# Windowed attention with a gated feed-forward block, fp16 on one core: global key rows copied in ahead of the DMA transposes, and a reordered head

## The chip, the cores and the metric

The kernel runs on one core of a Trainium2 chip. A core has five engines that run their own instruction streams and wait for each other through semaphores: TensorE (PE, with the weight loads shown apart as PEld), VectorE (DVE), ScalarE (ACT), GpSimd (POOL) and SyncE (SP). DMA transfers are issued by SP, ACT or POOL; those that POOL issues go through one queue (q0 in the profile) and those of SP through another (q1). The metric is the device time of one execution in microseconds. All times inside the execution are counted from the start of the profiled span.

## The reference

Inputs are `q`, `k`, `v` of shape (4, 8, 768, 64) in fp32 (batch, heads, sequence, head size), and the three weights of a gated feed-forward block. Each query attends to the 8 first ("global") keys and to the 96 latest ("local") keys, with a linear distance bias for each head:

```python
rel = pos[:, None] - pos[None, :]
is_global = pos[None, :] < 8
is_local = (rel >= 0) & (rel < 96)
keep = is_global | is_local
dist = np.where(is_global & ~is_local, 96.0, np.abs(rel))
scores = q @ k.T / 8 - slopes[:, None, None] * dist      # slopes 2**-(h+1)
a = softmax(np.where(keep, scores, -1e9))
x = (a @ v) as (4 * 768, 512)
out = (silu(x @ w_gate) * (x @ w_val)) @ w_out            # d_ff 1536
```

## The kernel before, in words

**Tiling.** The four batches are called blocks 0 to 3. A block has 768 tokens in two halves of 384; each half becomes one tile `x_of(t)` of the feed-forward stage, t = 0 to 7, in which x is held transposed (feature by token). The eight heads go as four pairs `hp`; two pairs make a quad. Keys are cut into 7 chunks of 120 with their window of 216 queries. A chunk's tile has 128 columns: columns 0 to 7 hold the 8 global keys, columns 8 to 127 the 120 local ones. V has the same layout in rows (`vSs[b]`, lines 120 and 158 to 162); its rows 0 to 7 of every chunk are copied in from `vG` by SP (`copy_globals`, lines 172 to 175).

**Attention.** For each pair K and Q are needed transposed (`kT`, `qT`). Block 0 and the pairs 0 and 1 of block 1 are transposed on PE and copied out of PSUM by DVE and ACT (`transposes_half`, line 284; `transposes`, line 258); pairs 2 and 3 of block 1 and all pairs of blocks 2 and 3 are loaded as rows into `kst` and `qst` by POOL (`load_rows`, line 181) and transposed by SP's DMA (`transposes_dma`, line 391), with the last 48 keys through `kend` and `kE` (`load_ends` 188, `turn_ends` 197). Before those loads `stage(b)` (line 143) zeroes on POOL the whole of `kend` and rows 0 to 7 of `kst`. After a DMA transpose `global_keys` (line 400) copies, on POOL, the transposed global keys into columns 0 to 7 of the pair's six chunks and of `kE`. Then PE makes scores, ACT the exponentials (lines 347 and 372), DVE or POOL multiplies by `masks` (380, 383), and `Quad.weigh` (line 428 onwards, matmuls at 435) makes denominators and numerators. DVE inverts and spreads the denominators (445 to 451), ACT copies the numerators out (466) and DVE (block 0) or POOL (other blocks) scales them into x (470; 491 in the head). The masks are sixteen exponentials on ACT (`make_masks`, line 242), of 432 or 216 columns.

**Feed-forward.** For each tile t and each of the 12 blocks f of 128 hidden units, `gate_or_val` (line 513) runs 4 gate matmuls, a tanh on ACT (519) and a fused (tanh + 1) * gate on DVE into `sl` (521), then 4 value matmuls and a multiply by `sl` on DVE (525). Their PSUM banks go round a ring of three, so that a value group takes over the bank of the gate group one f before, once `sl` has been read from it. `out_part` (line 529) does 3 of the 12 output matmuls of a 128-token row block; the fourth part is evicted by ACT (543, two buffers) and stored by SP (544).

**Order.** The schedule is written out by hand: the engines' streams are filled in program order and each engine runs its stream in that order. After a head (lines 587 to 645), which does half 0 of block 0, `stretches` (line 710) lists groups of feed-forward work (gate, value or output), and between them attention steps are dealt out evenly: each group adds its weight times a quota to `owed`, and when `owed` reaches 1 the next step runs. `half1` is the second half of block 0; `first(1)` the first half of block 1, beside tile 1; `both(1)` the second half of block 1 and the first of block 2, beside tiles 2 and 3. `at_step(t, f, ...)` hangs loads and masks ahead of a gate group. Functions put off (exponentials, masks, inversions, scalings) stand in `later` and are run at the following groups. `load_w(f0, f1)` (line 205) is four POOL issues whatever its width, `load_wo(g)` one issue of 512 KB, `load_qk(b)` two of 384 KB, `load_v_rest(b, c)` one of 120 KB.

Of the kernel before, what the change touches and what calls it, by code (L numbers as in the profile page):

```python
# [16 lines left out]
WIN = 216  # L17
# [20 lines left out]
def kernel(  # L38
# [104 lines left out]
    def stage(b):  # L143
        qst[b] = sb2.tile([128, NP * J * 2 * D], FP16, name="qst", tag="qst")
        kst[b] = sb2.tile([128, NP * J * 2 * D], FP16, name="kst", tag="kst")
        kend[b] = sb2.tile([128, H, D], FP16, name="kend", tag="kend", bufs=1)
        nc.gpsimd.memset(kend[b], 0.0)
        nc.gpsimd.memset(kst[b][0:NG, 768 * (0 if b > 1 else 2):], 0.0)

    def whole(st, b):  # L150
        return st[b][:, 0:NP * J * D].rearrange("p (h x) -> p h x", h=NP)
# [1 line left out]
    def load_qk(b):  # L153
        for st, src in ((kst, k), (qst, q)):
            nc.gpsimd.dma_start(
                out=whole(st, b), in_=src[b, 0:NP].rearrange("h (p j) d -> p h (j d)", p=128))
# [6 lines left out]


    vG = sb.tile([NG, B, H, D], FP16, name="vG")

    def load_globals():
        nc.gpsimd.dma_start(
            out=vG[:, 1:].rearrange("p b h d -> p (b h) d"),
            in_=v[1:, :, 0:NG, :].rearrange("b h p d -> p (b h) d"))  # L170

    def copy_globals(b):
        nc.sync.dma_start(
# [7 lines left out]
    def load_rows(b, i, h):  # L181
        st, src = ((qst, q), (kst, k))[i]
        p0, n = (0, 128) if st is qst else (NG, KC)
        nc.gpsimd.dma_start(  # L184
            out=rows_of(st, b, h // 2)[p0:p0 + n, :, h % 2, :],
            in_=src[b, h, 0:n * J].rearrange("(t p) d -> p t d", p=n))

    def load_ends(b):
        h0 = 2 * NP - len(by_dma(b)) * 2
        nc.gpsimd.dma_start(  # L190
            out=kend[b][NG:NG + S - KC * J, h0:, :],
            in_=k[b, h0:, KC * J:S, :].rearrange("h p d -> p h d"))

    def by_dma(b):
        return range(0 if b > 1 else 2, NP)
# [9 lines left out]
    def load_w(f0, f1):  # L205
        a, z = 128 * f0, 128 * f1
        for g in range(2):
            for w, src in ((wg, moe_w_gate), (wv, moe_w_val)):
                nc.gpsimd.dma_start(
                    out=w[:, 2 * g:2 * g + 2, a:z],  # L210
                    in_=src[256 * g:256 * g + 256, a:z].rearrange("(p s) f -> p s f", s=2))
# [30 lines left out]
    def make_masks(h, c0, c1):  # L242
        nc.scalar.activation(
            out=masks[:, h, c0:c1], in_=dist[:, c0:c1], func=AF.Exp, scale=-slopes[h])
# [8 lines left out]
    class Pair:  # L253
# [143 lines left out]
                    out=dst.rearrange("r (t p) -> r t p", t=J),  # L397
                    in_=rows_of(st, b, hp).rearrange("p t e d -> p (t e d)"))

        def global_keys(self):  # L400
            k3 = self.kT.rearrange("r (c m) -> r c m", m=128)
            first = k3[:, 0, NG:2 * NG]
            nc.gpsimd.tensor_copy(
                out=k3[:, 0:J, 0:NG], in_=first.unsqueeze(1).broadcast_to([128, J, NG]))
            nc.gpsimd.tensor_copy(out=kE[:, self.hp, 0:NG], in_=first)


    class Quad:

# [158 lines left out]
    def fill(n):  # L568

        for _ in range(n):  # L570
            nc.tensor.matmul(warm[:, 0:256], lhsT=ones[:, 0:128], rhs=ones[:, 0:256],
                             start=True, stop=True)

    def p_bias(hp, which, *tags):
        pairs[0, hp].sc = pairs[0, hp].bias(0, which, [single("sc", t) for t in tags])

    def p_sc(hp, which, *tags):
        if tags:
            p_bias(hp, which, *tags)
        pairs[0, hp].scores_half(0, which, pairs[0, hp].sc)  # L580

    def p_tr(hp, kt, qt, q_eng, n_fill=0):
        tr = [single("trs", t, FP16)[:, 0:TB] for t in (qt, kt)]
        pairs[0, hp].transposes_half(0, tr, V, q_eng, lambda: fill(n_fill))

    V, A = nc.vector.tensor_copy, nc.scalar.copy
    fill(14)
    A(out=q16[:, 0, 0:2], in_=q32)
    V(out=k16[:, 0, 0:2], in_=k32)
    for h in range(4):  # L590
# [3 lines left out]
    copy_globals(0)  # L594
    for h in range(4, 8):
        make_slope(nc.vector.tensor_scalar_mul, h)
    load_w(0, 4)
    load_w(4, 6)
    load_half(1, 0, H)
    load_w(6, 8)  # L600
# [1 line left out]
    for c in range(4, NCH):  # L602
        load_v_rest(0, c)
    load_w(10, 12)
    stage(1)
    load_qk(1)
    for g in range(3):
        load_wo(g)
    load_globals()
    for c in range(4):  # L610
        load_v_rest(1, c)
    load_ends(1)
    for hp in by_dma(1):
        for i in (1, 0):
            for e in range(2):
                load_rows(1, i, 2 * hp + e)
    for c in range(4, NCH):
        load_v_rest(1, c)
    p_bias(0, 0, "a0", "a1")
    sc00 = pairs[0, 0].sc  # L620
    p_bias(0, 1, "a2", "a3")
    pairs[0, 0].scores_half(0, 0, sc00)
    p_sc(0, 1)
    p_tr(1, "x2", "o0", V)
    p_bias(1, 0, "x0", "x1")
    p_tr(2, "a0", "a1", A)
    p_sc(1, 0)
    p_sc(1, 1, "x2", "o0")
    p_tr(3, "a2", "a3", A)
    p_sc(2, 0, "a0", "a1")  # L630
    quads[0, 0].denominators(single("den", "x0"))
    p_sc(2, 1, "a2", "a3")
    for side, tag in enumerate(("x1", "x2")):
        quads[0, 0].numerators(side, single("num", tag))
    p_sc(3, 0, "a0", "a1")
    p_sc(3, 1, "a2", "a3")
    quads[0, 1].denominators(single("den", "o0"))
    for side, tag in enumerate(("x0", "x1")):
# [33 lines left out]
    def second(b):  # L672
        return [[sc(b, 0, 2), sc(b, 1, 2)], [sc(b, 2, 2), sc(b, 3, 2)],
                [va(b, 0, 1)], [va(b, 1, 1)]]
# [6 lines left out]
                pairs[b, hp].transposes_dma()  # L681
        return step

    def gk(b, *hps):
        return lambda: [pairs[b, hp].global_keys() for hp in hps]

    def first(b):
        return [[tr(b, 0), tr(b, 1), fetch(b, 2, 3)], [sc(b, 0, 0), sc(b, 0, 1)],
                [sc(b, 1, 0), sc(b, 1, 1), gk(b, 2)], [va(b, 0, 0), gk(b, 3)],
                [sc(b, 2, 0), sc(b, 2, 1)], [sc(b, 3, 0), sc(b, 3, 1)], [va(b, 1, 0)]]  # L690

    def both(b):

        n = b + 1

        return [[sc(b, 0, 2), sc(b, 1, 2)], [sc(b, 2, 2), sc(b, 3, 2), fetch(n, 0, 1)],
                [va(b, 0, 1)], [va(b, 1, 1), gk(n, 0, 1)],
                [sc(n, 0, 0), sc(n, 0, 1), fetch(n, 2, 3)], [sc(n, 1, 0), sc(n, 1, 1)],
                [va(n, 0, 0), gk(n, 2, 3)], [sc(n, 2, 0), sc(n, 2, 1)],
                [sc(n, 3, 0), sc(n, 3, 1)], [va(n, 1, 0)]]  # L700

    half1 = [[trh(0), trh(1)], [trh(2), trh(3)], [sch(0)], [sch(1)],
# [4 lines left out]
    def ff(t, f0, f1, n_out=(0,)):  # L707
        return [(t, f, n_out[(f - f0) % len(n_out)]) for f in range(f0, f1)]

    stretches = [  # L710
        (ff(0, 0, 4), [], 0),
        (ff(0, 4, 12), half1, 1.0),
        (ff(1, 0, 3) + ff(1, 3, 12, (1, 1, 2)), first(1), 6.0),
        (ff(2, 0, 12, (1,)) + ff(3, 0, 12, (1,)), both(1), 6.0),
        (ff(4, 0, 12, (1,)) + ff(5, 0, 12, (1,)), both(2), 6.0),
        (ff(6, 0, 12, (1,)), second(3), 6.0),
        (ff(7, 0, 12, (1,)), [], 0)]

    loads = {}

    def at_step(t, f, *fns):
        loads.setdefault((t, f), []).extend(fns)

    for h in range(H):
        at_step(h // 4, 1 + h % 4, lambda h=h: make_masks(h, WIN, 3 * WIN))
        at_step(h // 4, (8, 1)[h // 4] + h % 4, lambda h=h: make_masks(h, 0, WIN))
    at_step(1, 0, lambda: [copy_globals(b) for b in range(1, B)])
    for b, base, rate, v_at in ((2, 24, 2.0, (30, 31, 32, 32, 37, 38, 39)), (3, 43, 1.4, (54, 55, 56, 57, 61, 62, 63))):
        items = [(base, lambda b=b: stage(b)), (base + 1, lambda b=b: load_ends(b))]
        n = 0  # L730
# [8 lines left out]
            at_step(int(when) // NFF, int(when) % NFF, it)  # L739

    outs = [(t, i, part) for t in range(NT - 1) for i in range(3) for part in range(4)]
    for tiles, steps, tail in stretches:
        groups = []
        for t, f, n_out in tiles:
            groups += [(1.0, t, f, which) for which in range(2)]
            groups += [(1.1, t, f, 2)] * n_out
        work = sum(g[0] for g in groups)
        quota = len(steps) / (work - tail)
        owed = 0.4
        for w, t, f, which in groups:  # L750
            if which == 0:
                for ld in loads.pop((t, f), []):
                    ld()
                if f == 0:
                    run_later(len(later))
            run_later(1)
            if which == 2:
                out_part(*outs.pop(0))
            else:
                gate_or_val(t, f, which, NC if t == 0 and f < 2 else 0)  # L760
            owed += w * quota
            while owed >= 1.0 and steps:
                run_later(len(later))
                for step in steps.pop(0):
                    step()
                owed -= 1.0
        assert not steps
    assert not later and not loads and not outs
    for i in range(2):
        for part in range(4):  # L770
            out_part(NT - 1, i, part)
# [36 lines left out]
```

The softmax here doesn't subtract the row's maximum and nothing guards it: scores larger than these inputs give would overflow.

## Time and profile before

| what | value |
|---|---|
| median of 13 runs | 255.2 us (252.77 to 257.93) |
| the profiled execution | 255.31 us, span 253.5 us, mean granted clock 0.993 |
| PE busy | 239.9 us, 95% of the span |
| DVE, ACT, POOL busy | 157.7, 129.8, 127.5 us |
| DMA moved | 25.76 MB, mean 102 GB/s; 81480 of 93251 packets under 512 B |
| issue to landing, median | V chunks 7.3, kst rows 4.3, qst rows 5.1, w_out 10.8, kT and qT transposes 5.7 and 6.6 us |

A line of PE's timeline gives start, duration, engine, source line, operation, the tile written and those read, shapes, how many instructions were merged, and in brackets how long the engine stood idle ahead of it and which event ended that. The durations of matmuls overlap, so work is better read from start to start. A DMA issue on POOL shows the time that POOL took to issue it; POOL can itself be held until earlier transfers of its queue have landed, and the bracket then names one of those. The table of stretches adds the granted TensorE clock (PEclk, 1.00 is full), the DMA engines' busy share and the bytes moved.

### The profile page before, as it was taken

The page shows a single profiled execution, that of the slowest core. Times are in us where ns is not written, and L with a number is a line of the kernel's source. Part 1 is how long each engine was busy: PE and PEld are TensorE (multiplying, and loading weights), DVE is VectorE, ACT ScalarE, POOL GpSimd, SP SyncE. Part 2 cuts the span into 40 slices and gives each one's busy share as a digit, 9 for nine tenths or more (in the row PEclk, how much of TensorE's full clock was granted, in tenths as well). Part 3 has the DMA queues.
Part 4 walks back from the last instruction along what each step waited for, and adds up shares of the span by engine and source line. Part 5 has one row for each costly group of instructions (what it writes and reads, how often), then busy time and mean ns, then how long its engine had stood idle before and what let it go on. Part 6 is the DMA issues. An engine that isn't in the chain of part 4 may idle for free.

```text
span 253.5 us, 6001 instructions
## 1 busy us (share of the span) xinstructions
PE 239.9 (95%) x2380; PEld 135.1 (53%) x2380; DVE 157.7 (62%) x338; ACT 129.8 (51%) x288; POOL 127.5 (50%) x161
## 2 busy tenths in 40 slices
PE   6989998989799999979999999999999999999994
PEld 4555565545355555544555555555555565555543
DVE  4577766557665666772675666766775567555510
ACT  4736676785453744543563554455734643332321
POOL 8975995490409998918808877813020232300000
PEclk9999999999999999997999999999999999999999
DMA  8999999999711999999934999991011101101122
GB/s 160 167 192 193 178 157 191 172 130 115 134 41 44 88 152 131 173 132 99 115 56 34 113 133 181 151 121 45 0 44 41 41 3 45 41 3 41 41 83 83
DMA packets 93251, 25.76 MB, mean 102 GB/s; under 512 B 81480, under 2 KB 90280, under 8 KB 93224
## 3 DMA queue, kind: packets, MB, share of 16 engines
q0 software_dynamic: 71088, 14.00, 74.5%
q1 hardware_dynamic: 21576, 11.03, 22.7%
q8 instruction: 18, 0.29, 0.5%
q10 hardware_dynamic: 560, 0.36, 0.5%
q14 instruction: 9, 0.07, 0.1%
HBM read 28.58 MB, written 6.29 MB: 138 GB/s over the span
## 4 chain that ended last, share of the span: by engine, by line
PE 70%; DMA 16%; ACT 5%; DVE 5%; issue 2%; POOL 0%; ACTq 0%; DVEq 0%; POOLq 0%
PE ops L537 20%; PE vps L508 19%; PE gps L508 19%; DMA vS<-in_v_dram 5%; DMA kT<-kst 4%; DMA qT<-qst 3%; PE sc L364 3%; PE num L435 3%; DMA vS<-vG 2%; DVE sl L521 2%; PE den L435 2%; DMA ident<-consts 1%; ACT at L372 1%; ACT th L519 1%; PE sc L328 1%
## 5 line engine op out<-in xcount | busy, mean ns | idle before, releaser
L521 DVE SCALAR_TENSOR_TENSOR sl<-th,gps 128x384 f32<-128x384 f32 x94 | 52.0, 553 | 57.4 <-ACT th L519 56.6
L519 ACT ACTIVATE th<-gps 128x384 f32<-128x384 f32 x94 | 46.6, 496 | 65.0 <-PE gps L508 63.4
L508 PE MATMUL gps<-xT,wg 128*128 128x384 f16 x376 | 77.6, 328 | 1.6 <-DVE xT L470 1.5
L508 PE MATMUL vps<-xT,wv 128*128 128x384 f16 x376 | 77.0, 327 | 1.5 <-DVE sl L521 1.5
L537 PE MATMUL ops<-wo,hT 128*128 128x512 f16 x276 | 73.7, 382 | 0.0
L525 DVE TENSOR_TENSOR hT<-vps,sl 128x384 f16<-128x384 f32 x94 | 51.9, 552 | 9.0 <-PE vps L508 2.0
L508 PEld LDWEIGHTS <-wg 128*128 128x128 f16 x384 | 36.7, 98 | 34.8 <-issue 4.1
L508 PEld LDWEIGHTS <-wv 128*128 128x128 f16 x384 | 36.6, 98 | 27.4 <-issue 3.7
L470 POOL TENSOR_TENSOR xT<-ns,rb 128x384 f16<-128x384 f32 x24 | 24.2, 1027 | 48.2 <-DVE rb L451 47.0
L372 ACT ACTIVATE at<-sc 128x432 f16<-128x432 f32 x72 | 33.3, 534 | 11.5 <-PE sc L364 11.5
L537 PEld LDWEIGHTS <-hT 128*128 128x128 f16 x276 | 26.0, 98 | 23.9 <-issue 1.2
L160 POOL DMA_DIRECT2D vS<-in_v_dram x28 | 24.9, 899 | 1.1 <-issue 1.1
L543 ACT ACTIVATE osb<-ops 128x512 f32<-128x512 f32 x23 | 13.7, 597 | 17.7 <-PE ops L537 17.7
L184 POOL DMA_DIRECT2D kst<-in_k_dram x20 | 17.7, 900 | 4.1 <-DMA wo<-in_moe_w_out_dram 4.1
L466 ACT COPY ns<-num 128x384 f32<-128x384 f32 x28 | 12.0, 482 | 12.7 <-PE num L435 12.7
L383 DVE TENSOR_TENSOR at<-at,masks 128x864 f16<-128x864 f16 x20 | 13.0, 650 | 7.8 <-ACT at L372 7.8
L184 POOL DMA_DIRECT2D qst<-in_q_dram x20 | 17.2, 881 | 0.0
L435 PE MATMUL num<-at,vS 128*32 128x216 f16 (+6 forms) x576 | 12.5, 225 | 2.1 <-DMA vS<-in_v_dram 1.9
L383 POOL TENSOR_TENSOR at<-at,masks 128x864 f16<-128x864 f16 x4 | 7.3, 1820 | 13.3 <-ACT at L372 13.3
L347 ACT ACTIVATE at<-sc 128x432 f16<-128x432 f32 (+2 forms) x32 | 11.6, 451 | 2.9 <-PE sc L339 2.9
L435 PEld LDWEIGHTS <-vS 128*32 128x32 f16 x576 | 10.0, 95 | 2.7 <-DMA vS<-in_v_dram 2.4
L364 PE MATMUL sc<-qT,kT 64*128 64x216 f16 (+2 forms) x148 | 9.7, 249 | 1.4 <-DMA qT<-qst 1.4
(69 smaller groups left out, 173.7 us busy)
## 6 DMA issues: line engine op xcount, KB each, us to landing
out_dram<-osb SPq DMA_DIRECT2D x23, 256.0 KB, 2.8
vS<-in_v_dram POOLq DMA_DIRECT2D x24, 120.0 KB, 7.3
qst<-in_q_dram POOLq DMA_DIRECT2D x20, 96.0 KB, 5.1
kst<-in_k_dram POOLq DMA_DIRECT2D x20, 90.0 KB, 4.3
wo<-in_moe_w_out_dram POOLq DMA_DIRECT2D x3, 512.0 KB, 10.8
wg<-in_moe_w_gate_dram POOLq DMA_DIRECT2D x8, 128.0 KB, 7.2
wv<-in_moe_w_val_dram POOLq DMA_DIRECT2D x8, 128.0 KB, 7.2
wg<-in_moe_w_gate_dram POOLq DMA_DIRECT2D x2, 256.0 KB, 6.3
```

The costliest lines, as they stand in the source:

```text
L160: nc.gpsimd.dma_start(out=vSs[b][NG:NG + n, c, :, :], in_=v[b, :, KC * c:KC * c + n, :].rearrange("h p d -> p h d"))
L184: nc.gpsimd.dma_start(out=rows_of(st, b, h // 2)[p0:p0 + n, :, h % 2, :], in_=src[b, h, 0:n * J].rearrange("(t p) d -> p t d", p=n))
L364: nc.tensor.matmul(sc[hi][:, col:col + n], lhsT=keys, rhs=self.qT[r, q0:q0 + n], start=True, stop=True)
L372: nc.scalar.activation(out=at[:, hi, :], in_=sc[hi][:, 0:BANK], func=AF.Exp, scale=scale)
L383: mul_eng.tensor_mul(at, at, m[:, :, o:o + BANK])
L435: nc.tensor.matmul(dst[r, o:o + n], lhsT=ones[:, 0:32] if side is None else vals[:, 4 * g + j, side::2], rhs=pairs[b, 2 * g + j // 2].at[c ...
L470: mul_eng.tensor_mul(self.x_out(half, side), srcs[side], self.rb)
L508: nc.tensor.matmul(gv[f, which][:, 0:TB], lhsT=w[:, c, 128 * f:128 * f + 128], rhs=x_of(t)[:, c, :], start=(c == 0), stop=(c == NC - 1))
L519: nc.scalar.activation(out=th, in_=dst[:, 0:TB], func=AF.Tanh, scale=0.5)
L521: nc.vector.scalar_tensor_tensor(out=sl, in0=th, scalar=1.0, in1=dst[:, 0:TB], op0=AluOp.add, op1=AluOp.mult)
L525: nc.vector.tensor_mul(hTs[t][:, f, :], dst[:, 0:TB], gv["sl"])
L537: nc.tensor.matmul(ops, lhsT=hTs[t][:, f, 128 * i:128 * i + 128], rhs=wo[:, f, :], start=(f == 0), stop=(f == NFF - 1))
```

## The change

1. `kG`, a tile like `vG`, is loaded by POOL with the global keys of blocks 1 to 3. `stage(b)` no longer zeroes rows 0 to 7 of `kst`; SP copies the global rows from `kG` into `kend` and, one DMA for each pair that is transposed by DMA, into those rows of `kst`. `global_keys` and its ten calls on POOL go.
2. In the head there are 17 instead of 14 filler matmuls; `load_w(0, 4)` becomes `load_w(0, 2)` and `load_w(2, 4)`; `load_wo` and `load_globals` go ahead of `stage(1)` and `load_qk(1)`; `load_ends(1)` and the rows of pair 2 go ahead of the first four V chunks of block 1. The transposes of pair 1 go ahead of the scores of pair 0, the q copy of pair 2 goes from ACT to DVE, and the first scores of pair 3 go ahead of the numerators of quad 0.
3. Four output groups (tile 0, first 128 tokens) come right after the last value group of tile 0, that is between `half1` and tile 1, and tile 1 has 8 output groups instead of 12. The start value of `owed` is now given for each stretch; the steps beside tile 1 come after 5 groups at first, where it was 3.
4. Each mask follows the tanh of a gate group, where it stood ahead of one; those of heads 4 to 7 are spread over f 0 to 5 of tile 1. `copy_globals` of blocks 1 to 3 moves from (1, 0) to (0, 10).

The few words given with the change also name whole V chunks; `load_v_rest` isn't in the diff.

```diff
         nc.gpsimd.memset(kend[b], 0.0)
-        nc.gpsimd.memset(kst[b][0:NG, 768 * (0 if b > 1 else 2):], 0.0)
+        nc.sync.dma_start(out=kend[b][0:NG], in_=kG[:, b])
+        for hp in by_dma(b):
+            pair = kG[:, b, 2 * hp:2 * hp + 2, :].rearrange("p h d -> p (h d)")
+            nc.sync.dma_start(
+                out=rows_of(kst, b, hp)[0:NG].rearrange("p t e d -> p t (e d)"),
+                in_=pair.unsqueeze(1).broadcast_to([NG, J, 2 * D]))
...
+    kG = sb.tile([NG, B, H, D], FP16, name="kG")
     def load_globals():
-        nc.gpsimd.dma_start(
-            out=vG[:, 1:].rearrange("p b h d -> p (b h) d"),
-            in_=v[1:, :, 0:NG, :].rearrange("b h p d -> p (b h) d"))
+        for dst, src in ((kG, k), (vG, v)):
+            nc.gpsimd.dma_start(
+                out=dst[:, 1:].rearrange("p b h d -> p (b h) d"),
+                in_=src[1:, :, 0:NG, :].rearrange("b h p d -> p (b h) d"))
...
-        def global_keys(self):
-            k3 = self.kT.rearrange("r (c m) -> r c m", m=128)
-            first = k3[:, 0, NG:2 * NG]
-            nc.gpsimd.tensor_copy(
-                out=k3[:, 0:J, 0:NG], in_=first.unsqueeze(1).broadcast_to([128, J, NG]))
-            nc.gpsimd.tensor_copy(out=kE[:, self.hp, 0:NG], in_=first)
...
-    fill(14)
+    fill(17)
...
-    load_w(0, 4)
+    load_w(0, 2)
+    load_w(2, 4)
     load_w(4, 6)
...
     load_w(10, 12)
-    stage(1)
-    load_qk(1)
     for g in range(3):
         load_wo(g)
     load_globals()
+    stage(1)
+    load_qk(1)
+    def load_pair(b, hp):
+        for i in (1, 0):
+            for e in range(2):
+                load_rows(b, i, 2 * hp + e)
+    load_ends(1)
+    load_pair(1, 2)
     for c in range(4):
         load_v_rest(1, c)
-    load_ends(1)
-    for hp in by_dma(1):
-        for i in (1, 0):
-            for e in range(2):
-                load_rows(1, i, 2 * hp + e)
+    load_pair(1, 3)
     for c in range(4, NCH):
         load_v_rest(1, c)
     p_bias(0, 0, "a0", "a1")
-    sc00 = pairs[0, 0].sc
-    p_bias(0, 1, "a2", "a3")
-    pairs[0, 0].scores_half(0, 0, sc00)
-    p_sc(0, 1)
     p_tr(1, "x2", "o0", V)
+    p_sc(0, 0)
+    p_sc(0, 1, "a2", "a3")
     p_bias(1, 0, "x0", "x1")
-    p_tr(2, "a0", "a1", A)
+    p_tr(2, "a0", "a1", V)
...
     p_sc(2, 1, "a2", "a3")
+    p_sc(3, 0, "a0", "a1")
     for side, tag in enumerate(("x1", "x2")):
         quads[0, 0].numerators(side, single("num", tag))
-    p_sc(3, 0, "a0", "a1")
...
     stretches = [
-        (ff(0, 0, 4), [], 0),
-        (ff(0, 4, 12), half1, 1.0),
-        (ff(1, 0, 3) + ff(1, 3, 12, (1, 1, 2)), first(1), 6.0),
-        (ff(2, 0, 12, (1,)) + ff(3, 0, 12, (1,)), both(1), 6.0),
+        (ff(0, 0, 4), [], 0, 0),
+        (ff(0, 4, 11) + [(0, 11, 4)], half1, 5.4, 0.4),
+        (ff(1, 0, 12, (0, 1, 1)), first(1), 6.0, -0.1),
+        (ff(2, 0, 12, (1,)) + ff(3, 0, 12, (1,)), both(1), 6.0, 0.4),
...
     for h in range(H):
-        at_step(h // 4, 1 + h % 4, lambda h=h: make_masks(h, WIN, 3 * WIN))
-        at_step(h // 4, (8, 1)[h // 4] + h % 4, lambda h=h: make_masks(h, 0, WIN))
-    at_step(1, 0, lambda: [copy_globals(b) for b in range(1, B)])
+        for (t, f), c0, c1 in zip((((0, h), (0, 8 + h)), ((1, h - 4), (1, h - 2)))[h // 4],
+                                  (WIN, 0), (3 * WIN, WIN)):
+            after_gate.setdefault((t, f), []).append(
+                lambda h=h, c0=c0, c1=c1: make_masks(h, c0, c1))
+    at_step(0, 10, lambda: [copy_globals(b) for b in range(1, B)])
...
                 gate_or_val(t, f, which, NC if t == 0 and f < 2 else 0)
+                for fn in after_gate.pop((t, f), []):
+                    fn()
```

More of the change, by code (lines that the diff above doesn't have):

```diff
@@ L682, in fetch @@
         return step
-    def gk(b, *hps):
-        return lambda: [pairs[b, hp].global_keys() for hp in hps]
     def first(b):
         return [[tr(b, 0), tr(b, 1), fetch(b, 2, 3)], [sc(b, 0, 0), sc(b, 0, 1)],
-                [sc(b, 1, 0), sc(b, 1, 1), gk(b, 2)], [va(b, 0, 0), gk(b, 3)],
+                [sc(b, 1, 0), sc(b, 1, 1)], [va(b, 0, 0)],
                 [sc(b, 2, 0), sc(b, 2, 1)], [sc(b, 3, 0), sc(b, 3, 1)], [va(b, 1, 0)]]
@@ L696, in both @@
         return [[sc(b, 0, 2), sc(b, 1, 2)], [sc(b, 2, 2), sc(b, 3, 2), fetch(n, 0, 1)],
-                [va(b, 0, 1)], [va(b, 1, 1), gk(n, 0, 1)],
+                [va(b, 0, 1)], [va(b, 1, 1)],
                 [sc(n, 0, 0), sc(n, 0, 1), fetch(n, 2, 3)], [sc(n, 1, 0), sc(n, 1, 1)],
-                [va(n, 0, 0), gk(n, 2, 3)], [sc(n, 2, 0), sc(n, 2, 1)],
+                [va(n, 0, 0)], [sc(n, 2, 0), sc(n, 2, 1)],
                 [sc(n, 3, 0), sc(n, 3, 1)], [va(n, 1, 0)]]
@@ L710 @@
     stretches = [
-        (ff(0, 0, 4), [], 0),
-        (ff(0, 4, 12), half1, 1.0),
-        (ff(1, 0, 3) + ff(1, 3, 12, (1, 1, 2)), first(1), 6.0),
-        (ff(2, 0, 12, (1,)) + ff(3, 0, 12, (1,)), both(1), 6.0),
[L715 to L719, printed above, removed]
+        (ff(0, 0, 4), [], 0, 0),
+        (ff(0, 4, 11) + [(0, 11, 4)], half1, 5.4, 0.4),
+        (ff(1, 0, 12, (0, 1, 1)), first(1), 6.0, -0.1),
+        (ff(2, 0, 12, (1,)) + ff(3, 0, 12, (1,)), both(1), 6.0, 0.4),
+        (ff(4, 0, 12, (1,)) + ff(5, 0, 12, (1,)), both(2), 6.0, 0.4),
+        (ff(6, 0, 12, (1,)), second(3), 6.0, 0.4),
+        (ff(7, 0, 12, (1,)), [], 0, 0)]
+    loads, after_gate = {}, {}
     def at_step(t, f, *fns):
@@ L741 @@
     outs = [(t, i, part) for t in range(NT - 1) for i in range(3) for part in range(4)]
-    for tiles, steps, tail in stretches:
+    for tiles, steps, tail, owed in stretches:
         groups = []
@@ L748 @@
         quota = len(steps) / (work - tail)
-        owed = 0.4
         for w, t, f, which in groups:
@@ L767 @@
         assert not steps
-    assert not later and not loads and not outs
+    assert not later and not loads and not after_gate and not outs
     for i in range(2):
```

## The prediction

> **What bounds the kernel now.** I read the page's engine table and chain first (PE busy 95% of 253.5 us, 70% of the chain, DMA 16%), then the busy time by stretches, then PE's timeline, looking for starts that come later than the pace. From 119 us to the end PE never pauses; up to there it does, and all that can be won lies there. PE's timeline, columns start, duration, instruction, and in brackets the idle time ahead of it and what ended it:
>
> ```profile
> 42.80 0.49 PE L508 MATMUL gps<-xT,wg 128*128 128x384 f16 x2
> 44.76 0.79 PE L508 MATMUL gps<-xT,wg 128*128 128x384 f16 x2 [1.47 <-DVE xT L470]
> ...
> 50.29 0.81 PE L508 MATMUL gps<-xT,wg 128*128 128x384 f16 x4
> 52.12 0.81 PE L508 MATMUL vps<-xT,wv 128*128 128x384 f16 x4 [1.02 <-DVE sl L521]
> ...
> 63.44 0.81 PE L508 MATMUL vps<-xT,wv 128*128 128x384 f16 x4
> 65.69 0.55 PE L364 MATMUL sc<-qT,kT 64*128 64x216 f16 x8 [1.44 <-DMA qT<-qst]
> ...
> 112.10 0.26 PE L435 MATMUL num<-at,vS 128*32 128x216 f16 x4
> 113.24 0.28 PE L435 MATMUL num<-at,vS 128*32 128x216 f16 x4 [0.88 <-DMA vS<-in_v_dram]
> 114.18 0.25 PE L435 MATMUL num<-at,vS 128*32 128x144 f16 x4 [0.66 <-DMA vS<-in_v_dram]
> 114.81 0.52 PE L435 MATMUL num<-at,vS 128*32 128x24 f16 x20 [0.39 <-DMA vS<-in_v_dram]
> 115.26 1.46 PE L537 MATMUL ops<-wo,hT 128*128 128x512 f16 x3
> ```
>
> The durations are pipelined, so I price a stall by starts: a group of 4 gate or 3 output matmuls starts 0.65 us after the one ahead (in the chain's list they follow at 0.65). (a) 44.76-42.80 less two matmuls (0.33): 1.64 lost to xT of tile 1. (b) 52.12-50.29-0.65 = 1.18, to sl. (c) 65.69-63.44-0.74 = 1.51, to a DMA transpose. (d) The denominators at 59.22 and 72.05 lead to num 0.96 and 1.22 later, where 0.28 is the pace (111.82 to 112.10): 0.68+0.94 = 1.62. (e) 115.26-112.10 = 3.16, where 0.66 is usual (73.27 to 73.93): 2.50, to V rows of block 2. And (f), in the stretches (columns: busy time per engine, granted clock, DMA share, GB/s):
>
> ```profile
> core 0: us, PE busy (x) PEld busy (x) DVE busy (x) ACT busy (x) POOL busy (x), PEclk, DMA share, GB/s
> 34.00:36.00 2.00, 2.00 (x67) 1.49 (x58) 1.40 (x4) 1.67 (x5) 2.00 (x4) 1.00 0.88 104
> 36.00:39.00 3.00, 3.00 (x32) 1.87 (x30) 2.75 (x6) 2.28 (x7) 3.00 (x5) 1.00 1.32 200
> ...
> 115.30:118.70 3.40, 3.40 (x17) 1.49 (x12) 0.14 (x1) 1.17 (x3) 3.02 (x4) 0.53 0.75 132
> ```
>
> Right after the V wait the granted clock is 0.53 for 3.4 us: groups start at 115.26, 116.52, 117.80, 118.80, so three take 3.54 instead of 1.95: 1.59 lost. (a) to (f) are 10.0 us. The head (to 24.7 us) loses time too, but POOL's and PEld's timelines show what stands behind it:
>
> ```profile
> 23.20 0.71 POOL L209 DMA_DIRECT2D wg<-in_moe_w_gate_dram  x1 [1.87 <-DMA k<-in_k_dram]
> ...
> 24.88 0.23 PEld L292 LDWEIGHTS <-q 128*64 128x64 f16 x6
> 24.94 0.71 POOL L209 DMA_DIRECT2D wv<-in_moe_w_val_dram  x1 [1.03 <-DMA q<-in_q_dram]
> ```
>
> POOL is released by the landing of half 1's q at 24.94, and PE's transposes of it begin at 24.88: q lands just when PE asks.
>
> **Part by part.**
>
> *Head: reordered transposes, 17 fillers, w(0,4) in two.* Moving p_sc(3,0) ahead of the numerators lets its exponentials start when those of pair 2 end (13.57) and not at 14.61; the q copy of pair 2 goes from ACT to DVE (0.48 against 0.55) and there delays pair 2's bias. I get 0.4 to 1.0 us at the end of the head. Three more fillers of 0.23 us (14 took 3.17) end at 5.04, when ident lands (1.26+3.77 = 5.03): free, and they may bring the fast matmuls (six transposes take 0.53 us at 8.28, 0.36 at 9.62) sooner. All of it runs into q's landing at 24.9: the queue moves 157 to 193 GB/s in every stretch up to there. Four more weight issues of 0.71 us put half 1's loads (13.91 and 15.18) 2.8 us later. They land 9.0 and 9.5 us after issue, where loads of the same 384 KB at 32.73 and 33.48 take 4.9 and 6.1: 3.4 to 4.1 us of that is queueing, more than the 2.8. From both sides: gain 0 (q's landing); loss 2.8, if all of the issue time is passed on. I take 0, by those landings.
>
> *Tile 0 to tile 1: four output groups at (0,11).* They fill (a): xT is ready at 44.15+1.03 = 45.2; the groups take 4*0.65 = 2.6 from 42.80, to 45.4. The cover holds if wo is there. In before the three wo loads release POOL at 43.10, 46.05 and 48.66, behind load_qk's 768 KB (3.9 us at 194 to 200 GB/s) and a lull (104 GB/s in 34 to 36: 0.9 us lost, while POOL did its memsets, 0.54+1.37). With wo ahead of both: 38.3, 41.2, 43.9, and the last is first used at 42.8+1.3+0.4 = 44.5. Gain 1.64, slack 0.6. load_qk pays: it now ends where wo ended, less 0.9, plus 0.2 for the new 24 KB of kG: 47.9. Its transposes move from the third to the fifth group of tile 1, to 45.4+5*0.65 = 48.7: slack 0.8.
>
> *Masks after the tanh.* (b)'s tanh stood behind two masks (ACT 50.21, 0.89 for two), but also behind 3.0 us of transposed copies (47.34 to 50.37). The copies stay, so I take 0.7 of 1.18. Against it: tile 1 has 4 output groups less (2.6 us of PE) for the same ACT work, and both mask sets fall into f 0 to 5; the denominators in (d) wait for the exponentials behind that. I add 0.3 to (d); at the ends, (d) vanishes (-1.6) or doubles (+1.6).
>
> *load_pair(1,2) ahead of four V chunks.* 480 KB fewer ahead of it (3.1 us at 154 GB/s, the rate of 47 to 52), and load_qk and wo together end 0.9 earlier. The transpose of (c) was issued at 57.26 and landed at 65.56; some 4 us sooner it is there before sc asks. Gain 1.51; next late is pair 3, issued at 62.30 at the latest in before and wanted 3.2 us after pair 2; it stays behind the same bytes.
>
> *Global key rows by SP; no kst memset, no copies on POOL.* POOL loses 2.65 us (78.86) ahead of block 2's loads and five waits for kT (13.5 us in all) with copies of 0.27+0.21 us. The loads start 2.65 earlier and POOL issues them without a break to 95. The queue then holds a backlog up to the V chunks (issue to landing 12.6 us at 102.21), so an earlier start is passed on, except what contention eats. Price of the new copies: 4 of 12 KB and one of 8 KB on SP, of a kind with vS<-vG (56 KB, 0.69 us of issue each, 5.30 us to land in a busy stretch): 3.5 us of SP, 0.3 of queue. They wait on kG (landing some 44) and the kend memset; behind them on SP stand copy_globals, outputs (two buffers, some 9 us apart) and turn_ends, none due before 49. Bounds for (e): nothing passed on, 0; all, 2.5. I take 2.65-0.3 less 0.25 for contention = 2.1, nearest to the backlog row; 0.4 of wait is left. With that short a wait (f) should go too: waits of 1.47 and 1.44 us left the clock at 1.00. Gain 1.59; at the other end 0.
>
> "TensorE: Matmul & The Clock Gate" (the Trainium skill, Part 1) has the clock fall after an idle window of about 3.4 us; here it fell to 0.53 after 0.88+0.66+0.39 us of waits with work between, so by that rule (f) would not have been there, and by the trace it goes only if most of (e) does. Against the copies, "DMA: Bandwidth & Descriptors" (Issuing engines are not separate DMA queues) says that SP's transfers run on the same engines as POOL's; no row separates this for so small a copy.
>
> *V chunks whole:* the diff leaves load_v_rest as it is; 0.
>
> **Sum,** against the profiled run of 255.31 (span 253.5; the median of the runs is 255.2): 1.64+0.7+1.51-0.3+2.1+1.59 = 7.2, so 248.1.
>
> **Rivals.** B: the V wait stays. POOL reaches block 2's loads only after xT of block 1's second quad (76.50 to 78.39), which in the shorter tile 1 may stand closer to tile 2's start, and a scaling at 95.11 waits for DVE, so that the last loads issue no sooner than now. Then (e) and (f) stay: 3.5 gained, 251.8. For it: xT gates POOL twice; against: the backlog at 102. C: wo or load_qk is late. Slack is 0.6 and 0.8; if they come 2 us late PE waits 1.3 and the clock may fall (1.6): 248.1+2.9 = 251.0, with B 254.7. D, the slower side: POOL's loads into kst wait for SP's copies into the same tile. load_qk would be issued at kG's landing (44) plus 0.69 plus some 4 (between ident's 3.8 and 5.30) = 48.7, and land 6.1 later than its second issue, at 56: 7 us after PE wants it, with 1.6 of slow clock, against 3.5 saved: 260.4. It decides as soon as load_qk is issued after 41. Against: copy_globals(0) was issued at 7.67, while the V chunks issued from 4.39 to 8.05, into other rows of the same tile, were still landing. E: the change does little, since the waits of tile 1 reappear as waits on ACT: (d) doubles and (b) stays: 250.4 at best and, with B, 254.1.
>
> **Chances.** Forecast 0.58; B 0.19; C 0.09; D 0.06; E 0.08. The forecast's low end: (d), the rest of (b) and of (e) vanish, 248.1-2.6 = 245.5. Upwards the range takes in B, C, E and reaches 254.0; D and the double cases are left out. About 0.5% (1.3 us) is what a measurement here can tell from no change: faster is under 253.9: the forecast, B, most of C and E, 0.86; same 0.06; slower 0.08.
>
> **What would show it.** Right: no xT wait near 45, four ops groups there without a pause; sc of pair 2 unreleased by a DMA; tile 2 starting some 3.5 us earlier than 78.48; num of block 2 with under 0.7 us of waits and a granted clock of 1.00 after it; PE still held by q at 24.9. Wrong: ops released by wo, trs by kst or qst, POOL released by kst<-kG, a DMA wait at num of block 2 with a clock near 0.5 behind it, or denominators that wait over 2 us on DVE's masks.

## The result and the profile after

The changed kernel takes 252.3 us in the median where the kernel before takes 255.58 beside it: a ratio of 0.9884, 95% interval [0.9846, 0.9921], so 1.2% or 3 us faster. 248.1 was forecast. Run again (e15) it gave 0.9899 [0.9851, 0.9946]. The profiled execution is 251.63 us (span 249.8) against 255.31 (253.5). The ratios leave out the slower executions into which a kernel falls now and then; in e2, e4 and e13 the profiled execution is one of these, so only the stretches named are read from those profiles.

PE's timeline of the changed kernel, the lines that answer to those shown of before (start, duration, instruction, idle time ahead of it and what ended it):

```profile
24.66 0.36 PE L299 MATMUL trs<-ident,k 128*64 128x128 f16 x6 [1.11 <-DMA k<-in_k_dram]
26.71 0.36 PE L299 MATMUL trs<-ident,q 128*64 128x128 f16 x6 [1.69 <-DMA q<-in_q_dram]
...
44.05 1.89 PE L537 MATMUL ops<-wo,hT 128*128 128x512 f16 x8
46.65 1.02 PE L537 MATMUL ops<-wo,hT 128*128 128x512 f16 x4 [0.71 <-DMA wo<-in_moe_w_out_dram]
47.51 0.81 PE L508 MATMUL gps<-xT,wg 128*128 128x384 f16 x4
...
57.58 0.81 PE L508 MATMUL vps<-xT,wv 128*128 128x384 f16 x4 [0.59 <-DVE sl L521]
...
67.06 0.55 PE L371 MATMUL sc<-qT,kT 64*128 64x216 f16 x8 [1.20 <-DMA qT<-qst]
...
70.60 0.55 PE L371 MATMUL sc<-qT,kT 64*128 64x216 f16 x8 [0.93 <-DMA qT<-qst]
...
112.24 0.42 PE L435 MATMUL num<-at,vS 128*32 128x216 f16 x12
113.09 0.47 PE L435 MATMUL num<-at,vS 128*32 128x24 f16 x20 [0.43 <-DMA vS<-in_v_dram]
113.49 0.82 PE L537 MATMUL ops<-wo,hT 128*128 128x512 f16 x3
```

The stretches of the same execution (busy time per engine, granted clock, DMA share, GB/s; the DMA share goes above 1 where the times of the packets add up to more than the stretch):

```profile
19.00:23.00 4.00, 3.51 (x22) 2.02 (x21) 3.58 (x8) 2.66 (x7) 3.49 (x6) 1.00 1.26 148
...
115.30:118.70 3.40, 3.40 (x25) 1.75 (x24) 2.23 (x4) 1.45 (x4) 3.40 (x5) 1.00 0.25 80
```

Two halves are to be seen. **Block 2** went as forecast: num starts at 112.24 as it did at 112.10, the waits for V have shrunk from 1.93 us to 0.43, and the clock behind them is 1.00. From 112.24 to the fourth group behind num it is 3.2 us where it was 6.7. That, less 0.14 us by which num starts later, is 3.4 of the 3.7 us that the execution gained. **All ahead of it** gave next to nothing: tile 2's first gate group starts at 78.31, where it started at 78.48. The xT wait (1.47) is gone, but half 1's q, which landed as PE asked for it, now lands about 2 us later than before, and PE waits for half 1's k (1.11) and q (1.69), for w_out (0.71) and for the DMA transposes of pairs 2 and 3 (1.20 and 0.93). POOL's timeline shows q's landing, 26.95 where it was 24.94:

```profile
24.90 0.71 POOL L216 DMA_DIRECT2D wg<-in_moe_w_gate_dram  x1 [1.09 <-DMA k<-in_k_dram]
26.95 0.71 POOL L216 DMA_DIRECT2D wv<-in_moe_w_val_dram  x1 [1.34 <-DMA q<-in_q_dram]
```

### The profile page after: what moved, and what is told of

It reads as the page before. It is cut to its first block, busy times and chain, and to the rows that moved or that the text cites. A ratio compares the mean times of both kernels' runs of the same rounds, so it can differ in the third digit from the quotient of the medians.

```text
span 249.8 us, 5993 instructions
## 1 busy us (share of the span) xinstructions
PE 236.7 (95%) x2383; PEld 133.8 (54%) x2383; DVE 156.5 (63%) x339; ACT 129.5 (52%) x287; POOL 119.8 (48%) x143
## 4 chain that ended last, share of the span: by engine, by line
PE 62%; DMA 20%; POOL 9%; ACT 3%; issue 2%; DVE 2%; POOLq 0%
PE ops L537 20%; PE gps L508 17%; PE vps L508 17%; DMA vS<-in_v_dram 7%; DMA qT<-qst 5%; DMA wo<-in_moe_w_out_dram 5%; DMA q<-in_q_dram 3%; PE sc L371 3%; POOL vS L165 2%; PE num L435 2%; POOL wv L216 2%; PE den L435 1%; POOL xT L470 1%; POOL wg L216 1%; PE ops L553 1%
## 5 line engine op out<-in xcount | busy, mean ns | idle before, releaser
L508 PE MATMUL gps<-xT,wg 128*128 128x384 f16 x376 | 76.8, 326 | 0.1
L470 POOL TENSOR_TENSOR xT<-ns,rb 128x384 f16<-128x384 f32 x24 | 23.5, 996 | 68.5 <-DVE rb L451 68.5
L390 DVE TENSOR_TENSOR at<-at,masks 128x864 f16<-128x864 f16 x20 | 12.1, 607 | 7.9 <-ACT at L379 7.9
```

Of the source, the lines that this page charges most:

```text
L390: mul_eng.tensor_mul(at, at, m[:, :, o:o + BANK])
L470: mul_eng.tensor_mul(self.x_out(half, side), srcs[side], self.rb)
L508: nc.tensor.matmul(gv[f, which][:, 0:TB], lhsT=w[:, c, 128 * f:128 * f + 128], rhs=x_of(t)[:, c, :], start=(c == 0), stop=(c == NC - 1))
```

## The experiments

Ratios are to the kernel before, run beside each on the same chip, five rounds each; in brackets the 95% interval.

### e1: the weights whole again

```diff
-    load_w(0, 2)
-    load_w(2, 4)
+    load_w(0, 4)
```

> The changed kernel with load_w(0, 4) in one piece again (four POOL issues instead of eight). Theory (issue time): the four extra issues of 0.71 us let POOL's queue run dry ahead of half 1, whose q lands at 26.7 instead of 24.9, and the 1.8 us are passed on to all that follows. Then PE's first transposes of half 1's q start near 24.9, tile 2 some 1.8 us earlier than 78.3, the waits for w_out (0.71) and for the DMA transposes (1.20 and 0.93) shrink too, and the time is 1.8 to 3.5 us under that of the changed kernel, 249 to 250.5 us against 255.6 for before. Rival (the head itself): PE only asks for half 1 earlier, and q lands late for another reason (the order of the head, the global loads): q still at 26 or later and the time within 0.5 us of the changed kernel, 252.3.

Measured: 250.91 us, 0.9829 [0.975, 0.9908]. PE's starts that waited for a DMA:

```profile
25.49 0.36 PE L299 MATMUL trs<-ident,q 128*64 128x128 f16 x6 [1.69 <-DMA q<-in_q_dram]
45.55 1.02 PE L537 MATMUL ops<-wo,hT 128*128 128x512 f16 x4 [0.83 <-DMA wo<-in_moe_w_out_dram]
65.63 0.55 PE L371 MATMUL sc<-qT,kT 64*128 64x216 f16 x8 [0.83 <-DMA qT<-qst]
70.39 0.55 PE L371 MATMUL sc<-qT,kT 64*128 64x216 f16 x8 [2.17 <-DMA qT<-qst]
```

q comes 1.2 us sooner than in the changed kernel, so the split is part of the cause; of the 1.8 us by which PE starts on q later than before (24.93), 0.6 stay. But PE runs into the transposes all the same: what was won ahead of 65 us is waited away at pairs 2 and 3. The ratio is 0.5% better than the changed kernel's, with overlapping intervals.

### e2: the split alone, on the kernel before

```diff
-    load_w(0, 4)
+    load_w(0, 2)
+    load_w(2, 4)
```

> The kernel before with nothing changed but load_w(0, 4) in two pieces. Issue time: half 1's q lands some 1.8 us later (26.5 to 27), PE waits 1.5 to 2 us there, and w_out and the rows of block 1 come as much later: 1.8 us slower or more, 257 to 258.5 us; the wait for V of block 2 stays, as loads of block 2 start after tile 1's end. Rival: no more than 0.4 us slower, since the loads stood in a queue anyway (which is what the prediction counted).

Measured: 1.0036 [0.9991, 1.008]. q releases POOL at 25.90 instead of 24.94. The split delays the same load in the old head too, by 1.0 us against before and by 0.4 to 1.0 against the six profiles of the old head without it (24.9 to 25.5); the cost to the whole, 0.4%, isn't clear of zero and lies nearer to the rival's 0.4 us than to the 1.8 expected.

### e13: the split's POOL time without the split

```diff
     load_w(0, 4)        # on e1
+    for _ in range(3):
+        nc.gpsimd.memset(idle[0:NG], 0.0)     # an unused tile of 1024 columns
```

> The changed kernel with load_w(0, 4) whole, and behind it 2.94 us of unused memsets on POOL (three of 8 rows of 1024 into a tile that nothing reads), about the time of the four issues that the split adds (4*0.71 = 2.85). If the split costs by POOL's issue time, half 1's q lands as late as in the changed kernel, 26 to 26.7, and the time is that of the changed kernel, 1 to 1.5 us over the one with the whole load_w (250.9 where the changed kernel has 252.3). If it costs by the narrower pieces (512 B instead of 1 KB a row, some 180 instead of 192 GB/s), q lands at 25.1 to 25.9 and nothing is lost.

Measured: 250.33 us, 0.9772 [0.9716, 0.9829]. Its seven executions lie between 248.49 and 255.07 us, so it can't be told apart from e1. POOL issues k and q of half 1 at 16.63 and 17.51, nearly as late as in the changed kernel (17.30 and 18.18):

```profile
10.89 2.94 POOL L600 MEMSET idle<- 8x1024 f16 x3
...
16.63 0.89 POOL L118 DMA_DIRECT2D k<-in_k_dram  x1
17.51 0.89 POOL L118 DMA_DIRECT2D q<-in_q_dram  x1
...
25.61 0.71 POOL L217 DMA_DIRECT2D wv<-in_moe_w_val_dram  x1 [1.33 <-DMA q<-in_q_dram]
```

q lands at 25.61, no later than with the whole load_w alone (25.74). So the issue time by itself isn't what costs. With the split the queue moves less from 12 to 19 us: 177 to 186 GB/s in its four profiles with the new head (the changed kernel's, e4, e14, e15), 192 to 198 in the six without it (e13 among them). First the changed kernel, then e13:

```profile
12.00:19.00 7.00, 6.04 (x111) 3.58 (x111) 4.41 (x9) 2.45 (x8) 6.38 (x9) 1.00 1.38 180
```

```profile
12.00:19.00 7.00, 6.51 (x113) 3.74 (x113) 4.88 (x10) 3.02 (x9) 6.94 (x9) 1.00 1.28 196
```

My theory for e1 and e2, the queue running dry for want of issues, fails as the only cause in the new head; there the narrower pieces (two transfers of 128 KB for one of 256) remain, by elimination, as what makes q late. From 19 to 23 us the queue moves 148 to 163 GB/s with the split, 174 in e13 and 187 to 191 in the other five, so there the issue time has a share in the dip, though not enough to delay q. For the old head this isn't shown: e2 moves 190 GB/s in 12 to 19 us, hardly under the 192 of before, and only 176 for 192 in 19 to 23 us, so what delays its q by 1.0 us stays open.

### e3 and e12: the copies alone

The kernel before with part 1 of the change only (both global loads stand ahead of `stage(1)`, which the copies need); e12 is the same kernel on another chip.

```diff
-        nc.gpsimd.memset(kst[b][0:NG, 768 * (0 if b > 1 else 2):], 0.0)
+        nc.sync.dma_start(out=kend[b][0:NG], in_=kG[:, b])
+        for hp in by_dma(b):
+            nc.sync.dma_start(out=rows_of(kst, b, hp)[0:NG]..., in_=pair...)
...
-    stage(1)
+    load_globals()      # kG and vG
+    stage(1)
```

> The kernel before with the global key copies alone: kG loaded by POOL (both global loads ahead of the staging of block 1), SP's copies in place of the kst memset and of POOL's copies after the transposes; head, weights, output groups and masks as before. Theory: the shorter wait for V of block 2 and the full clock after it, 2.1 and 1.6 us, are the whole of what the change won, so this gives 3 to 4 us, 251.5 to 252.5 us, with num of block 2 waiting under 0.7 us and a granted clock of 1.00 behind it. Rival: the wait went because tile 1 is arranged otherwise, and here it stays with the slow clock: 255 to 256 us.

> The kernel before with the global key copies alone, once more, on the chip of the other three. If the copies alone win 1.5% as in the first run (0.9853), the further edits of the change together cost about 0.3% net; if it is nearer to 0.990, they cost nothing, and the difference lay between chips.

Measured: 0.9853 [0.9794, 0.9912] and 0.9852 [0.9813, 0.9892], 250.88 and 250.97 us. In e3's profile PE has no wait left at block 2 (in e12's 0.58 us):

```profile
64.89 0.55 PE L371 MATMUL sc<-qT,kT 64*128 64x216 f16 x8 [0.48 <-DMA qT<-qst]
...
111.30 0.77 PE L435 MATMUL num<-at,vS 128*32 128x216 f16 x32
```

The copies alone win as much as the whole change or 0.3 to 0.5% more (the intervals overlap); the other three parts together gave nothing. They weren't tested one by one.

### e4: the memset's time put back

```diff
         nc.gpsimd.memset(kend[b], 0.0)
+        if b > 1:
+            for _ in range(3):
+                nc.gpsimd.memset(idle[0:NG], 0.0)
```

> The changed kernel with 2.7 us of unused memsets on POOL (three of 8 rows of 1024, into a tile that nothing reads) in the staging of blocks 2 and 3, where the kst memset stood. Theory: the memset's POOL time was the cause of the wait for V of block 2; the loads start 2.7 us later, the wait grows from 0.6 to over 2 us and the slow clock may come back: 1.5 to 3.5 us slower than the changed kernel, 254 to 256 us. Rival: the copies after the transposes were the cause (POOL held by kT ahead of the V loads): within 0.5 us of the changed kernel, 252.3.

Measured: 0.9989 [0.9935, 1.0043], 255.4 us: all of the change's gain is gone, for 2.9 us of POOL per block in which nothing else changes. PE's waits for V of block 2 are back:

```profile
117.56 0.28 PE L439 MATMUL num<-at,vS 128*32 128x216 f16 x4 [1.43 <-DMA vS<-in_v_dram]
118.37 0.25 PE L439 MATMUL num<-at,vS 128*32 128x144 f16 x4 [0.53 <-DMA vS<-in_v_dram]
119.28 0.72 PE L439 MATMUL num<-at,vS 128*32 128x24 f16 x20 [0.66 <-DMA vS<-in_v_dram]
```

So the memset's time ahead of the loads is enough to cost all of it, with POOL's waits for kT still gone.

### e5, e6, e7: what holds up the transposes of block 1

On e1: V chunks 0 to 3 ahead of pairs 2 and 3 again (e5), the global loads directly behind half 1's (e6), both (e7).

```diff
-    load_ends(1)                 # e5, e7
-    load_pair(1, 2)
     for c in range(4):
         load_v_rest(1, c)
+    load_ends(1)
+    load_pair(1, 2)
     load_pair(1, 3)
...
     load_half(1, 0, H)           # e6, e7
+    load_globals()
     load_w(6, 8)
...
-    load_globals()
     stage(1)
```

> The changed kernel with load_w(0, 4) whole and the four V chunks of block 1 ahead of pairs 2 and 3 again, as before. In the kernel with only the whole load_w, PE waits 0.83 and 2.17 us for the DMA transposes of pairs 2 and 3. Theory 1 (load order): pair 2's transposes, made early, run among the row loads of pair 3 and the V chunks, which then move at half their rate, so pair 3 comes later; with V first the two waits fall from 3.0 to under 1.5 us in sum and the time by 1 to 2 us, to 0.976 to 0.981 of before. Theory 2 (SP's own late work: copies of global rows at 46 to 50 and the first output at 51): the waits stay at 2 to 3.5 us and the time within 0.5 us of the kernel with only the whole load_w (0.983).

> The changed kernel with load_w(0, 4) whole and load_globals directly behind half 1's loads, so that kG and vG land some 15 us earlier and SP's eight copies are done before 42. Theory 2 (SP's late copies stand ahead of the transposes and among the row loads): kE and the transposes of pair 2 are issued 2 to 3 us sooner than 51.7 and 54.9, the waits for pairs 2 and 3 fall from 3.0 to under 1.5 us, 1 to 2 us faster than with the whole load_w alone (0.976 to 0.981 of before). Theory 1 (load order): the wait for pair 3 stays near 2 us and the time within 0.5 us (0.983).

> The two edits together: load_w(0, 4) whole, V chunks first, globals early. Both theories: transpose waits under 1 us in sum, w_out's wait stays at 0.8; 2 to 3 us faster than with the whole load_w alone, 0.972 to 0.977 of before. If the waits stay over 2 us, neither is the cause, and the first output store or the transposes themselves are.

Measured: 0.9837 [0.9772, 0.9902], 0.9997 [0.9963, 1.003] and 0.9947 [0.9916, 0.9977]. The transposes' waits fell to 0.26, 0 and 0 us, yet none of the three is faster than e1. PE just waits ahead of them, for w_out at the four output groups: 1.97 us in e5, 0.53+3.45 in e6, 3.73 in e7, with 3.4 us (e6: 6.8 us) of slow clock around or behind it. Both theories expected a gain and neither got it: what one transfer wins another loses. Why w_out lands later in these three isn't shown.

### e8: copies and masks

On e3, each mask behind the tanh (part 4 without the move of `copy_globals`).

```diff
-        at_step(h // 4, 1 + h % 4, lambda h=h: make_masks(h, WIN, 3 * WIN))
-        at_step(h // 4, (8, 1)[h // 4] + h % 4, lambda h=h: make_masks(h, 0, WIN))
...
+            after_gate.setdefault((t, f), []).append(
+                lambda h=h, c0=c0, c1=c1: make_masks(h, c0, c1))
```

> The kernel before with the global key copies and, as the only other edit, each mask behind the tanh. Theory: value groups of tile 1 wait 1.0 us for sl because the tanh stood behind two masks; with masks behind it the wait falls to about 0.4 and the kernel is 0.5 to 0.8 us faster than with the copies alone (0.982 to 0.983 of before, against 0.9853). Rival: the copies out of PSUM on ACT hold the tanh anyway, and the masks only move to where the denominators wait: within 0.3 us of the copies alone.

Measured: 0.9932 [0.989, 0.9973], if anything slower than the copies alone, which neither the theory nor its rival foresaw. The wait for sl fell from 1.01 to 0.30+0.31 us, as expected, and PE came to pair 2's scores sooner and waited there until 65.41:

```profile
51.21 0.81 PE L508 MATMUL vps<-xT,wv 128*128 128x384 f16 x4 [0.31 <-DVE sl L521]
65.41 0.55 PE L371 MATMUL sc<-qT,kT 64*128 64x216 f16 x8 [2.36 <-DMA qT<-qst]
```

In the thirteen profiles with all V chunks of block 1 ahead of 66 us pair 2's scores start at 64.9 us or later: up to 67.4 in eight of them, at 68.0 and 68.4 in e15 and e13, and at 70.0 to 70.4 in e4, e6 and e7. No order of the same transfers got under 64.9.

### e9, e10, e11, e14: fewer transfers ahead of the transposes

The last three V chunks of block 1, which aren't wanted before the second half of block 1 (the denominators at 91.5), are loaded from the middle of tile 1: on e3 (e9), e8 (e10), e1 (e11) and the changed kernel itself (e14).

```diff
-    for c in range(4, NCH):
-        load_v_rest(1, c)
...
+    at_step(1, 8, lambda: [load_v_rest(1, c) for c in range(4, NCH)])
```

> The kernel before with the global key copies, and the last three V chunks of block 1 (wanted from 91 us on only) loaded from the middle of tile 1, at (1, 8), so that they are not in the queue while the DMA transposes of pairs 2 and 3 run. Theory (one full queue): the transfers up to the transposes fill the DMA engines from 2 to 66 us, so no order of the same transfers brings the transposes sooner, only fewer transfers do; the transposes of pair 2 land 1 to 3 us sooner than 64.8 and their wait (0.48 in the profile of the copies alone) is gone; 0 to 0.8 us faster than the copies alone. Rival: the DMA transposes take 7 to 9 us whatever runs beside them: no change in their landing.

> The same with each mask behind the tanh. With the copies and masks alone PE waited 2.36 us for the transpose of pair 2, with a slow clock after it. One full queue: the wait falls under 0.5 us, the clock stays at 1.00, and what the masks won (0.7 us at 51) is kept: 0.5 to 1.5 us faster than the copies with late V alone and 2 to 3 us faster than copies and masks (253.1). Rival: the wait stays near 2 us.

> The changed kernel with load_w(0, 4) whole and the last V chunks of block 1 from (1, 8). One full queue: of the two transpose waits (0.83 and 2.17 us) under 1 us is left, no slow clock at 70, 2 to 3 us faster than with the whole load_w alone (250.9), 248 to 249. Rival: the waits stay at 2 to 3 us, 250.5 to 251.5.

> The changed kernel with the last three V chunks of block 1 loaded from (1, 8) and nothing else: load_w stays split. With both repairs the changed kernel gave 248.55 (0.9764). If the split's 1.2 us are lost only where PE waits for q, this is 1 to 1.5 us slower than that, 249.5 to 250.5; if w_out's wait and the transposes come late again behind it, 251 or more.

Measured: 0.9786 [0.9747, 0.9826], 0.9774 [0.9737, 0.9811], 0.9764 [0.9713, 0.9814], 0.98 [0.9748, 0.9852]; 249.5, 249.31, 248.55 and 249.87 us. PE's scores of pairs 2 and 3 in e9, with no wait in brackets:

```profile
64.12 0.54 PE L371 MATMUL sc<-qT,kT 64*128 64x216 f16 x8
67.30 0.54 PE L371 MATMUL sc<-qT,kT 64*128 64x216 f16 x8
```

and the stretch in which the transposes run, first in e9, then in e12 (same kernel, V not late); the last two columns are DMA share and GB/s:

```profile
55.00:66.00 11.00, 10.81 (x111) 5.76 (x110) 7.64 (x17) 7.30 (x17) 4.38 (x6) 1.00 1.35 142
```

```profile
55.00:66.00 11.00, 9.05 (x98) 4.82 (x98) 7.13 (x16) 5.68 (x13) 6.76 (x8) 1.00 1.85 143
```

PE is busy 10.81 of 11 us instead of 9.05 (10.33 in e3's profile of that kernel, where it waited 0.48 us for pair 2, not 1.76). The three chunks stand behind the rows of pairs 2 and 3 in POOL's order, so it isn't by their place that they hold anything up. But beside them the q transpose of pair 2 let PE start 7.3 to 7.8 us after its issue on SP (e3, e8, e12); without them PE found it landed 6.8 us after issue in e9 and 5.2 us in e10 and didn't wait. That speaks against e9's rival, that a transpose takes 7 to 9 us whatever runs beside it. A wait of 0.36 us for pair 3 is left in e10.

With this edit and the whole load_w (e11) the changed kernel's other parts do their work too: no wait for w_out, none for a transpose, tile 2 at 75.17. e11 is the fastest kernel here, 2.4% under before, and all four beat both given kernels in the median; among the four the intervals overlap, so neither the masks (e10) nor the new head (e11) is shown to add anything to e9. e14, with the split left in, waits again for w_out (1.16) and for pair 3 (0.86).

### e15: the changed kernel again

> The changed kernel itself once more, on the chip of the other two, as their base: 0.985 to 0.992 of before.

Measured: 0.9899 [0.9851, 0.9946], 252.42 us; waits for q (1.68) and for both transposes (2.06 and 0.79) as in the first profile, none for w_out.

## Why the prediction was right or wrong, point by point

The side was right, the size wrong: 7.2 us forecast, 3.7 in the profiled execution, 3.2 to 3.3 in the medians. Two steps failed most, both on transfers: the early load of pair 2, booked as a gain of 1.51 us, lost 0.76, and the split head, taken at 0, cost 1.25 by the end of tile 0. Term by term, in us gained:

| term | forecast | profiled execution |
|---|---|---|
| head | 0 | -1.25 |
| (a) output groups | 1.64 | 0.78 |
| (b) masks | 0.7 | 0.43 |
| (c) transposes of pairs 2 and 3 | 1.51 | -0.76 |
| (d) denominators | -0.3 | 0.66 |
| (e) V of block 2 | 2.1 | 1.91 |
| (f) slow clock behind it | 1.59 | 1.59 |

The last column adds up to 3.4; 0.3 us of the gain is left unassigned. The measured time lies inside the stated range and within 0.5 us of rival B's 251.8, but by chance: B's V wait did not stay.

- **Head: wrong.** The step "Four more weight issues ... I take 0, by those landings" looked for the cost in POOL's issue time. That part holds in the new head (e13: as much POOL time, q no later). What it left out is that with two transfers of half the width the queue moved less there: 180 against 192 to 198 GB/s, and q came 1.2 us later (the changed kernel against e1). PE's start on q is 1.8 us later than before, and 1.25 us of that is left where tile 0's last value group ends (44.05 for 42.80). The bound of the step (up to 2.8) would have held both. With the split taken back q still lands at 25.3 to 26.2 in the kernels with the new head and at 24.9 to 25.5 with the old one; what makes that difference stays open.
- **Output groups at (0,11): mechanism right, size half.** xT's wait is gone; 44.05 to 47.51 is 3.46 us for four groups, so 0.86 lost where 1.64 was. w_out's last load released POOL at 46.89, not 43.9: the slack was put at 0.6 us, and q's delay in the head, 1.8 us, is three times that. This is rival C, at 0.7 us instead of 1.3.
- **Masks after the tanh: right in kind.** sl's wait fell from 1.02 to 0.59, so 0.43 was gained where 0.7 of 1.18 was forecast, and (d) went from 1.62 to 0.96 lost, better than the 0.3 added. In e8 the wait fell by 0.40 us, and that was worth nothing by itself, since pair 2's scores come next.
- **load_pair(1,2) ahead of V: wrong, the largest miss.** The step "some 4 us sooner it is there before sc asks" failed: the transpose of q of pair 2 was issued at 57.80 (57.26 before) and its scores started at 67.06 (65.69). Both transposes cost 2.27 instead of 1.51. The rows did come sooner, if by 2 to 2.6 us and not 4: issue plus time to landing gives 52.9 for the last of k and some 55 for the last of q, where it was 55.5 and 57.1. But SP, which issues the transposes, was taken by then: from kG's landing at 47.26 (the prediction said some 44) it issued the copies of the global rows, an output store and kE, each within 0.2 us of the end of the one before:

```profile
47.26 0.67 SPq L148 DMA_DIRECT2D kend<-kG  x1
...
49.57 2.26 SPq L180 DMA_DIRECT2D vS<-vG  x3
...
53.43 2.83 SPq L206 DMA_TRANSPOSE kE<-kend  x1
56.45 1.24 SPq L403 DMA_TRANSPOSE kT<-kst  x1
57.80 1.33 SPq L403 DMA_TRANSPOSE qT<-qst  x1
```

  The prediction priced this time of SP's (3.5 us) but found nothing due behind it before 49. In e6, where the copies end at 41.2, kT and qT of pair 2 are issued at 54.27 and 55.61, within 0.4 us of the landing of their rows. The second part is pair 3, of which the prediction said that it stays behind the same bytes. I counted bytes ahead of the load and not the transfers beside it: its rows took 7.7 us to land before, 8.8 to 11.9 in the changed kernel, 10.5 to 11.9 in e1, and 7.0 to 8.4 in e11, where the three chunks issued behind them are gone; the q transpose went out at 67.41 (62.30 before; 61.30 in e11). e5 to e8 move waits about and win nothing; e9 to e11 take three chunks out, and of the waits only 0.36 us in e10 is left. So the transfers up to 66 us get in each other's way whichever engine issues them. The Trainium skill's page "DMA: Bandwidth & Descriptors" (Issuing engines are not separate DMA queues) says that transfers issued by SP and by POOL run on the same DMA engines; the prediction weighed it for the small copies only, where e3, with the copies over by 41.1 us, shows no harm to the time, and not for the transposes.
- **Global copies: right.** 2.1 forecast for (e), 1.9 measured; e3 and e4 show the cause from both sides. Rivals B, D and E did not happen.
- **(f): right in this execution, less in the mean.** The clock after num is 1.00. But the granted clock over an execution (0.993 with the one slow window of before's profile) shows that such windows came in only some executions of before: of 29 beside e5, twelve with 0.997 or more took 252.5 to 254.0 us, the others with 0.993 or less took 254.7 and up, some 2 us more for the window and what goes with it. The changed kernel has such windows too: of six executions in e15 one had 1.00, the others 0.986 to 0.993, and in e15's profile the clock is 0.58 in 26 to 30 us, behind the wait for q. e3 (six) and e10 (six) have none, at 0.999 or more.

## What to carry to other kernels

When the DMA engines are full for the first quarter of a kernel, a wait for a transfer may not go by reordering the transfers: here PE ran into the next one that landed late each time. Where one engine issues copies and transposes in turn, count its own time as well: a load that lands sooner gains nothing while that engine is busy. Look for bytes in that stretch that nobody wants yet, and move them out; here taking three V chunks out gave more than the head, the masks and the output groups together. Price a load that is cut in two by what it moves per microsecond as well as by its issues, and read a load that lands "just when asked" as a floor under everything ahead of it.

## What the runs showed of the hardware that was not expected

- With the first weights loaded in pieces of 128 KB the queue moved 177 to 186 GB/s in 12 to 19 us (four profiles with the new head), with pieces of 256 KB 192 to 198 (six profiles). With the old head it was 190 (e2) against 191 to 198 (six profiles).
- Waits of less than 2 us were followed by some 3.4 us at about half the granted clock (before: 0.88+0.66+0.39 us, then 0.53), and in e6, with 3.98 us of waits, by two such windows (0.60 and 0.50 from 46.0 to 52.9 us); of the same kernel some executions have it and others not. In e11's profile it followed a single wait of 1.69 us for q (0.57 in 26 to 30 us), in the changed kernel's profile waits of 1.11 and 1.69 us had no slow clock behind them (1.00 in 26 to 30 us).
